# Local-global attention with a gated feed-forward: gate by min(exp, 1), global normalising on ScalarE, later last products, second buffers, weights by block

## The chip, the cores and the metric

One core of one Trainium2 chip runs the kernel. The metric is the device time of one execution, in microseconds (us). Engines are called as in the profile: PE (TensorE matmul), PEld (its weight loads), DVE (VectorE), ACT (ScalarE), POOL (GpSimd), SP (SyncE, which issues the DMAs here).

## The reference

Batch 8, 8 heads, 512 local tokens, 32 global tokens, head dimension 64; then a gated feed-forward (512 to 1536 to 512) on the 8 x 544 rows.

```python
k_all = np.concatenate([k_g, k_l], axis=2); v_all = np.concatenate([v_g, v_l], axis=2)
out_g = np.matmul(sm(scale * np.matmul(q_g, k_all.transpose(0, 1, 3, 2))), v_all)   # global rows see all keys
s_ll = np.where(np.abs(pos[:, None] - pos[None, :]) <= 32, scale * q_l @ k_l^T, -1e9)
s_l = np.concatenate([scale * q_l @ k_g^T, s_ll], axis=-1)                          # local rows: 32 global keys + a band
out_l = np.matmul(sm(s_l), np.concatenate([v_g, v_l], axis=2))
x = concat([out_g, out_l], axis=2) as (B*S, H*D)
gate = 1.0 / (1.0 + np.exp(-(x @ w_gate))); val = x @ w_val
return gate * val @ w_out
```

## The kernel before

The work is cut into chunks of tokens: two half chunks of 256 tokens for batch element 0, seven chunks of 512 for the others, and last the 256 global rows of all batch elements. `ffn_stream` is the backbone. It walks over items, one for each chunk and each of the 12 blocks of 128 hidden columns. An item is 12 matmuls into `bank_g`, 12 into `bank_v` (both L370; weights and x are split into a high and a low part, and three of the four products are taken), the gate, and one item later the matmuls into `bank_o0` to `bank_o3` (L404). The generator yields after every four matmuls; between yields a queue of events, sorted by due time, issues the attention of the next chunk and, in the first 200 us or so, the conversion of the weights from 64-bit words (`convert`, L125 to L135).

The attention of a chunk goes head by head. A head has two `local_unit`s and one `global_unit`. A local unit takes scores on PE (L229, `bank_x`), mask and row maximum on DVE (L241), exp on ACT (L244), the scaling by 1/sum (L210 or L208), transposes on PE (L260, L261, `bank_y`), a copy into `pt` (ACT L270 for the high part, DVE L271 for the low part), and the product with v on PE (L287, L288), which ACT L290, DVE L291 and POOL L292 add up. In the first chunks, where the data are not split, the copy is `pt_nat` or `pt_first` (L267) and the result is copied by L283. `x_split` (L352, L353) then makes the two parts of x. A global unit takes 32 x 512 scores (L322), min and exp (L328, L331), 1/sum (L333, L334), the scaling of `pg` (L335), five transposes on DVE (L336, L339) into `ptg`, and a split (ACT L344, POOL L345). The five products with v (L300) of a head are issued inside the next head's global unit, one after each score matmul; those of the last head of a chunk have an event of their own.

All four of `bank_g`, `bank_v`, `bank_x` and `bank_y` share four PSUM buffers (tag `att`), so PE waits for whoever read the buffer last.

The gate uses sigmoid(g) = (1 + |tanh(g/2)|) * exp(min(g, 0)) / 2:

```python
nc.scalar.activation(th, acc, AF.Tanh, scale=0.5)
nc.vector.tensor_scalar(mn, acc, 0.0, None, op0=ALU.min)   # in 12 early items Relu on ACT
nc.scalar.activation(mn, mn, AF.Exp)
nc.scalar.activation(th, th, AF.Abs)
```

The order on each engine is fixed when the program is built; the scheduler that sorts ready instructions works from the due times.

## Time and profile before

| | |
|---|---|
| median of 3 runs | 1273.19 us (1268.44 to 1275.16) |
| profiled execution, its own time | 1267.32 us |
| its span | 1265.5 us |
| mean granted TensorE clock | 0.972 |
| busy in the span | PE 94%, PEld 77%, DVE 67%, ACT 60%, POOL 47% |

A wait is printed as "engine tile line <- releaser: us in total, times, longest". In a timeline row the columns are start and duration in us, engine, line, operation, tiles and shapes, count, and in brackets the idle time just before it with what ended it. In the table of windows each engine has busy us and, in brackets, the number of its instructions.

### The profile page before, as it was taken

The numbers are of one execution on the slowest core, as the hardware profiler recorded it, in microseconds if no ns is written. First come the engines' busy times: TensorE is split into PE (matmuls) and PEld (weight loads), VectorE is DVE, ScalarE is ACT, GpSimd is POOL, SyncE is SP. The second block draws the span as 40 slices with busy tenths as digits, with TensorE's granted clock in tenths as the row PEclk, the third lists the DMA queues.
The fourth block names the chain that finished last, engine by engine and source line by source line (L and its number), as shares of the span: only waits on it lengthen the run. The fifth ranks groups of instructions, "written<-read, shape, count | busy, mean of one in ns | idle before, by whom it ended". The sixth has DMA issues, their size and how long they took to land.

```text
span 1265.5 us, 19750 instructions
## 1 busy us (share of the span) xinstructions
PE 1185.2 (94%) x6500; PEld 971.9 (77%) x6500; DVE 849.2 (67%) x2525; ACT 758.7 (60%) x1740; POOL 593.9 (47%) x630
## 2 busy tenths in 40 slices
PE   5888979989999999999999999999999999999998
PEld 4656757878788778778887778877887888788897
DVE  3787896766777577757777577757775777622232
ACT  4555556665667567656676566656765666633243
POOL 1332454553555456554556355545655456411111
PEclk9688888989999999999999999999999999999999
DMA  5665674433333333333334333333333433121133
GB/s 201 202 208 192 234 237 122 124 94 111 90 116 104 121 101 109 92 118 114 85 115 129 114 100 118 92 121 102 108 92 118 133 94 103 36 98 67 67 134 117
DMA packets 59495, 152.81 MB, mean 121 GB/s; under 512 B 6144, under 2 KB 19456, under 8 KB 59392
## 3 DMA queue, kind: packets, MB, share of 16 engines
q1 hardware_dynamic: 59392, 151.54, 38.3%
q8 instruction: 51, 0.84, 0.3%
q14 instruction: 52, 0.43, 0.1%
HBM read 136.31 MB, written 15.20 MB: 120 GB/s over the span
## 4 chain that ended last, share of the span: by engine, by line
PE 57%; DVE 18%; issue 11%; ACT 8%; POOL 4%; DMA 1%; SPq 0%; POOLq 0%; ACTq 0%; DVEq 0%
PE bank_o L404 15%; PE bank_v L370 14%; PE bank_g L370 13%; PE bank_x L229 4%; ACT s_buf L244 2%; DVE t L291 2%; PE bank_x L322 2%; DVE ptg_buf L339 2%; DVE pg_buf L335 2%; PE bank_y L260 2%; DVE s_buf L210 2%; PE bank_y L261 1%; DVE r L252 1%; PE bank_x L300 1%; PE bank_x L287 1%
## 5 line engine op out<-in xcount | busy, mean ns | idle before, releaser
L370 PE MATMUL bank_g<-xt,wg 128*128 128x512 f32 (+1 forms) x1440 | 340.9, 372 | 4.5 <-ACT xt L352 4.5
L404 PE MATMUL bank_o<-wo,hh 128*128 128x512 f32 x1224 | 330.2, 402 | 6.9 <-ACT hh L390 4.5
L370 PE MATMUL bank_v<-xt,wv 128*128 128x512 f32 (+1 forms) x1440 | 330.2, 366 | 6.3 <-DVE pt L271 6.3
L370 PEld LDWEIGHTS bank_g<-xt,wg 128*128 128x128 f32 x1440 | 242.8, 194 | 48.1 <-ACT xt L352 7.1
L370 PEld LDWEIGHTS bank_v<-xt,wv 128*128 128x128 f32 x1440 | 238.8, 190 | 46.3 <-DVE pt L271 7.8
L391 POOL TENSOR_TENSOR hh<-th,hh 128x512 fp32r<-128x512 f32 (+1 forms) x120 | 138.1, 1151 | 263.8 <-ACT hh L390 257.1
L404 PEld LDWEIGHTS bank_o<-wo,hh 128*128 128x128 f32 x1224 | 219.7, 190 | 51.0 <-ACT hh L390 5.5
L244 ACT ACTIVATE s_buf<-s_buf,nm 128x192 f32<-128x192 f32 (+1 forms) x248 | 114.0, 461 | 53.3 <-DVE nm L241 49.9
L383 DVE TENSOR_SCALAR mn<-bank_g 128x512 f32<-128x512 f32 (+1 forms) x108 | 67.0, 620 | 117.6 <-ACT th L378 117.3
L191 POOL TENSOR_TENSOR kl<-qk_raw,qk_hi 128x736 fp32r<-128x736 f32 x52 | 92.2, 1772 | 113.6 <-ACT qk_hi L190 111.5
L390 ACT CAST hh<-th 128x512 fp32r<-128x512 f32 (+1 forms) x120 | 66.5, 554 | 101.2 <-DVE th L388 99.9
L292 POOL TENSOR_TENSOR x<-t 64x256 f32<-64x256 f32 x104 | 77.1, 741 | 85.0 <-DVE t L291 82.2
L378 ACT ACTIVATE th<-bank_g 128x512 f32<-128x512 f32 (+1 forms) x120 | 64.1, 534 | 85.6 <-PE bank_g L370 81.8
L241 DVE CUSTOM_DVE_ANT_0 s_buf<-bank_x,masks 128x192 f32<-128x192 f32 (+1 forms) x248 | 82.5, 366 | 30.4 <-PE bank_x L229 28.6
L387 DVE TENSOR_TENSOR bank_v<-bank_v,mn 128x512 f32<-128x512 f32 (+1 forms) x120 | 73.2, 610 | 42.8 <-PE bank_v L370 36.5
L252 DVE TENSOR_SCALAR r<-sm 128x2 f32<-128x2 f32 x128 | 44.8, 350 | 77.5 <-ACT s_buf L244 76.6
L203 POOL TENSOR_TENSOR vhl<-v_raw,vhl 128x512 fp32r<-128x512 f32 x52 | 67.3, 1294 | 35.7 <-ACT vhl L202 34.0
L193 POOL TENSOR_TENSOR qk_hi<-qk_raw,qk_hi 64x256 fp32r<-64x256 f32 x104 | 80.2, 786 | 7.4 <-ACT qk_hi L190 2.9
L210 DVE TENSOR_SCALAR s_buf<-s_buf,r 128x224 f32<-128x224 f32 (+1 forms) x230 | 78.5, 359 | 3.4
L190 ACT CAST qk_hi<-qk_raw 128x1280 fp32r<-128x1280 f32 x52 | 65.7, 1264 | 24.9 <-PE bank_x L300 15.6
L384 ACT ACTIVATE mn<-mn 128x512 f32<-128x512 f32 (+1 forms) x108 | 63.1, 584 | 29.2 <-DVE mn L383 26.1
L339 DVE STREAM_TRANSPOSE ptg_buf<-pg_buf 32x128 f32<-32x128 f32 x256 | 77.3, 302 | 4.0
(109 smaller groups left out, 2083.4 us busy)
## 6 DMA issues: line engine op xcount, KB each, us to landing
wo<-wo_dram SPq DMA_DIRECT2D x116, 512.0 KB, 3.3
qk_raw<-in_qk_dram SPq DMA_DIRECT2D x104, 320.0 KB, 4.6
v_raw<-in_v_dram SPq DMA_DIRECT2D x52, 256.0 KB, 2.6
out_dram<-ob SPq DMA_DIRECT2D x34, 256.0 KB, 2.3
xt<-in_w_gate_dram SPq DMA_DIRECT2D x12, 512.0 KB, 4.1
xt<-in_w_val_dram SPq DMA_DIRECT2D x12, 512.0 KB, 4.2
xt<-in_w_out_dram SPq DMA_DIRECT2D x12, 512.0 KB, 4.3
v_nat<-in_v_dram SPq DMA_DIRECT2D x8, 512.0 KB, 5.7
```

The lines of the kernel that those rows point to most:

```text
L191: nc.gpsimd.tensor_tensor(kl, t[:, K0:Q1], hi[:, K0:Q1].bitcast(F32), op=ALU.subtract)
L193: nc.gpsimd.tensor_tensor(hi[64:128, r], t[64:128, r], hi[64:128, r].bitcast(F32), op=ALU.subtract)
L203: nc.gpsimd.tensor_tensor(vhl[:, :, D:2 * D], t, vhl[:, :, 0:D].bitcast(F32), op=ALU.subtract)
L210: nc.vector.tensor_scalar(out, in_, by, None, op0=ALU.mult)
L241: anchor[0] = nc.vector.tensor_tensor_reduce(out=s_sb[:, i, 0:w], in0=s_ps[:, i, 0:w], in1=masks[:, m:m + w], scale=-0.125, scalar=3.0e38, ...
L244: nc.scalar.activation(s_sb[:, i, 0:w], s_sb[:, i, 0:w], AF.Exp, bias=nm[:, i:i + 1], scale=-1.0, accum_out=sm[:, i:i + 1])
L292: nc.gpsimd.tensor_tensor(dst, t0[:, :, 0], t0[:, :, 1], op=ALU.add)
L339: nc.vector.transpose(ptg32[SG * a:SG * a + SG, 0:4], src)
L370: nc.tensor.matmul(acc, w[a][:, t, fs], xt[:, c, t, x0:x0 + ntok], start=n == 0, stop=n == 11)
L387: nc.vector.tensor_tensor(acc, acc, mn, op=ALU.mult)
L391: nc.gpsimd.tensor_tensor(hh[:, 1, 0:ntok], th, hh[:, 0, 0:ntok].bitcast(F32), op=ALU.subtract)
L404: nc.tensor.matmul(o_ps[t], ph[:, a, t * P:(t + 1) * P], pwo[:, c], start=f2 == 0 and i == 0, stop=f2 == NF - 1 and i == 2)
```

## The change

- The gate: ACT takes exp(g) straight from `bank_g` (into `ex`), and the minimum with 1 is folded into the product with the value, so the DVE min (or the ACT Relu) goes.
- The scaling of `pg` in `global_unit` goes from DVE to ACT.
- The products of the last head of a chunk come 1.25 steps of `per` later.
- `th`, `ex` and `pt` get two buffers, `ob` four, `s_buf` three. The scratch for dynamic DMAs is cut to 1024 to make room.
- The weights are laid out by block on the host, so that a block is one contiguous piece of 4 KB for each partition instead of four of 1 KB (w_gate and w_val; w_out was so before).

```diff
-    s_bufs = [const.tile([P, 2, WIN], F32, name=f"s_buf{i}") for i in range(2)]
+    s_bufs = [const.tile([P, 2, WIN], F32, name=f"s_buf{i}") for i in range(3)]
...
+    w_src = [w[f] for f in range(NF) for w in (w_gate, w_val, w_out)]
...
-            nc.sync.dma_start(st, src)
+            nc.sync.dma_start(conv_bufs[0][i % len(conv_bufs[0])], w_src[i])
...
-            s_sb = ffn.tile([P, 2, WIN], F32, name="s_first", tag="ob", bufs=2)
+            s_sb = ffn.tile([P, 2, WIN], F32, name="s_first", tag="ob", bufs=4)
...
-            s_sb = s_bufs[cnt["s"] % 2]
+            s_sb = s_bufs[cnt["s"] % 3]
...
-            pt = att.tile([P, 2, 4, P], F32R, name="pt", bufs=1)
+            pt = att.tile([P, 2, 4, P], F32R, name="pt", bufs=2)
...
-        nc.vector.tensor_scalar(pg, pg, mg[:, 3:4], None, op0=ALU.mult)
+        nc.scalar.mul(pg, pg, mg[:, 3:4])
...
-                        th = ffn.tile([P, 512], F32, name="th", bufs=1)[:, 0:ntok]
-                        mn = ffn.tile([P, 512], F32, name="mn", bufs=1)[:, 0:ntok]
+                        th = ffn.tile([P, 512], F32, name="th", bufs=2)[:, 0:ntok]
+                        ex = ffn.tile([P, 512], F32, name="ex", bufs=2)[:, 0:ntok]
                         nc.scalar.activation(th, acc, AF.Tanh, scale=0.5)
-                        if n_it < 2 * NF and n_it % 2:
-                            nc.scalar.activation(mn, acc, AF.Relu, scale=-1.0)
-                            nc.scalar.activation(mn, mn, AF.Exp, scale=-1.0)
-                        else:
-                            nc.vector.tensor_scalar(mn, acc, 0.0, None, op0=ALU.min)
-                            nc.scalar.activation(mn, mn, AF.Exp)
+                        nc.scalar.activation(ex, acc, AF.Exp)
                         nc.scalar.activation(th, th, AF.Abs)
                     else:
-                        nc.vector.tensor_tensor(acc, acc, mn, op=ALU.mult)
+                        nc.vector.scalar_tensor_tensor(acc, ex, 1.0, acc, op0=ALU.min, op1=ALU.mult)
...
-                            ob = ffn.tile([P, DM], F32, name="ob", bufs=2)
+                            ob = ffn.tile([P, DM], F32, name="ob", bufs=4)
...
-            ev.append((start + per * npu * NH, 2, lambda: list(global_products(heads[NH - 1]))))
+            ev.append((start + per * (npu * NH + 1.25), 2, lambda: list(global_products(heads[NH - 1]))))
...
-    nc = bacc.Bacc("TRN2", target_bir_lowering=False, num_devices=1)
+    nc = bacc.Bacc("TRN2", target_bir_lowering=False, num_devices=1, dynamic_dma_scratch_size=1024)
```

In the changed program the same lines have other numbers: 6 lower up to the gate (L364 is L370, L281 is L287, L294 is L300, L264 is L270, L265 is L271, L329 is L335), L376 and L377 for L387 and L388, and 11 lower behind it (L393 is L404).

The order on PE at the end of a full chunk, where the last head's products stand. Before:

```order
L370 MATMUL bank_v<-xt,wv_113 128x512 x4
L370 MATMUL bank_v<-xt,wv_112 128x512 x4
L300 MATMUL bank_x<-ptg,vhl 128x64 x5
L287 MATMUL bank_x<-pt,vhl 128x256
L288 MATMUL bank_x<-pt,vhl 128x256
...
L404 MATMUL bank_o_6237<-wo,hh 128x512
L404 MATMUL bank_o_6238<-wo,hh 128x512
```

and now, at the same place:

```order
L364 MATMUL bank_v<-xt,wv_115 128x512 x4
L281 MATMUL bank_x<-pt,vhl 128x256
L282 MATMUL bank_x<-pt,vhl 128x256
...
L364 MATMUL bank_v<-xt,wv_114 128x512 x4
L393 MATMUL bank_o_6189<-wo,hh 128x512
...
L294 MATMUL bank_x<-ptg,vhl 128x64 x5
L364 MATMUL bank_g<-xt,wg_112 128x512 x4
```

The five products moved behind the twelve `bank_o` matmuls, and the last local product (L287) moved ahead of the last four `bank_v` matmuls.

The order on ACT for the same last head, from the exp of its global scores on. Before:

```order
L331 ACTIVATE pg_buf,sg<-pg_buf,mg 32x544
L290 COPY t_9054<-bank_x 64x512
L202 CAST vhl<-v_raw 128x8x64
L270 CAST pt<-bank_y 128x512
L378 ACTIVATE th<-bank_g 128x512
L385 ACTIVATE th<-th 128x512
L384 ACTIVATE mn<-mn 128x512
L344 CAST ptg<-ptg_buf 128x5x32
```

and now:

```order
L325 ACTIVATE pg_buf,sg<-pg_buf,mg 32x544
L284 COPY t_8985<-bank_x 64x512
L329 ACTIVATE pg_buf<-pg_buf,mg 32x544
L264 CAST pt<-bank_y 128x512
L196 CAST vhl<-v_raw 128x8x64
L372 ACTIVATE th<-bank_g 128x512
L373 ACTIVATE ex<-bank_g 128x512
L374 ACTIVATE th<-th 128x512
L338 CAST ptg<-ptg_buf 128x5x32
```

The scaling of `pg` came in ahead of the cast of `pt`, the cast of the next v moved behind it, and the exponential follows the tanh at once.

## The prediction

> **What bounds the kernel now.** I read the page first: busy shares, the granted clock in the 40 slices (tenths), the chain by engine.

> ```profile
> PE 1185.2 (94%) x6500; PEld 971.9 (77%) x6500; DVE 849.2 (67%) x2525; ACT 758.7 (60%) x1740; POOL 593.9 (47%) x630
> PEclk9688888989999999999999999999999999999999
> PE 57%; DVE 18%; issue 11%; ACT 8%; POOL 4%; DMA 1%; SPq 0%; POOLq 0%; ACTq 0%; DVEq 0%
> ```

> PE is the bound: idle for 80 us in all, and only in the first nine slices throttled. None of the matmuls is removed, so what can be won is PE's idle time and its slow clock. Next the windows, to see where both lie (first 200 us, the rest of the start, one full chunk, the end without attention):

> ```profile
> 31.00:200.00 169.00, 143.82 (x775) 106.92 (x776) 139.62 (x394) 98.05 (x256) 69.86 (x56) 0.82 0.63 209
> 200.00:284.00 84.00, 76.46 (x532) 67.27 (x533) 54.57 (x185) 54.39 (x147) 45.38 (x51) 0.96 0.40 112
> 557.00:694.00 137.00, 131.15 (x713) 108.28 (x714) 100.22 (x304) 89.86 (x198) 76.08 (x82) 1.00 0.37 110
> 1107.00:1212.00 105.00, 104.44 (x463) 85.15 (x464) 27.61 (x41) 33.15 (x55) 17.79 (x15) 1.00 0.22 75
> ```

> In 31 to 200 us DVE is busy 139.6 of 169 us, nearly as long as PE, and the clock is 0.82. A full chunk loses about 6 us of 137. Last, whom PE waits for, from 0 to 200 us:

> ```profile
> PE bank_y L260 <- DVE s_buf L210: 11.5, 7, 3.0
> PE bank_x L229 <- DMA qk_nat<-in_qk_dram: 9.2, 1, 9.2
> PE bank_x L300 <- DVE ptg_buf L339: 6.5, 5, 2.1
> PE bank_o L404 <- ACT hh L390: 4.3, 2, 3.1
> PE bank_o L404 <- POOL hh L391: 1.9, 3, 0.9
> ```

> and from 200 to 1107 us:

> ```profile
> PE bank_x L300 <- POOL ptg L345: 12.0, 7, 3.8
> PE bank_x L229 <- DVE t L291: 8.7, 14, 0.7
> PE bank_v L370 <- DVE pt L271: 6.3, 12, 0.8
> PE bank_x L322 <- DVE mn L383: 4.9, 8, 0.7
> PE bank_g L370 <- ACT xt L352: 3.8, 5, 1.0
> PE bank_x L287 <- DVE pt L271: 1.7, 3, 0.7
> ```

> These repeat chunk by chunk: seven waits for `ptg` are one for each chunk with a last head, fourteen for `t` two each. The change speaks to nearly every one.

> **The change, part by part.**

> *Last products later.* One chunk end, as it is:

> ```profile
> 690.22 0.69 DVE L271 TENSOR_TENSOR pt<-bank_y,pt 128x512 fp32r<-128x512 f32 x1
> 693.31 0.52 POOL L345 TENSOR_TENSOR ptg<-ptg_buf,ptg 128x160 fp32r<-128x160 f32 x1
> 693.89 0.74 PE L300 MATMUL bank_x<-ptg,vhl 128*128 128x64 f32 x5 [1.35 <-POOL ptg L345]
> 694.47 0.36 PE L287 MATMUL bank_x<-pt,vhl 128*128 128x256 f32 x1
> 695.03 2.91 PE L404 MATMUL bank_o<-wo,hh 128*128 128x512 f32 x12
> 699.33 0.50 PE L370 MATMUL bank_g<-xt,wg 128*128 128x512 f32 x1 [0.69 <-ACT xt L352]
> ```

> `ptg` is ready at 693.83; PE was there 1.35 us before 693.89, at 692.54. Now PE first does the four local products (694.47 to 695.03, 0.56) and the twelve `bank_o` (some 2.8), so it comes to the products at 695.9, 2 us after `ptg`. That covers the pass through ACT that the scaling adds. Late next would be `pt`: L287 is reached 0.93 earlier (four of the twelve matmuls of 2.8 us now stand behind it), at 691.6, and `pt` was ready at 690.91, so 0.7 us are left. All 12.0 us of these waits go. The longest, 3.8 us, also slowed the clock:

> ```profile
> 274.50:278.50 4.00, 0.16 (x1) 0.00 (x0) 2.03 (x5) 1.47 (x5) 3.78 (x5) 0.86 0.07 26
> 278.50:284.00 5.50, 5.49 (x23) 5.30 (x24) 0.90 (x2) 1.31 (x3) 2.68 (x4) 0.50 0.49 121
> ```

> 5.5 us at 0.50 are worth 2.7. Together 14.7. The step issues no DMA, so no queue but PE's is passed. [...]

> *The wait for `xt`* (3.8): the last L287 ends 2.5 to 3 us earlier against the next chunk's `bank_g`, since waits and products no longer stand ahead of it, and L290, L291, L292, L352 follow it. A wait of 0.69 goes with that: 3.8.

> *Scaling of `pg` on ACT.* Its price on both engines, the second row for the same shape on ACT:

> ```profile
> L335 DVE TENSOR_SCALAR pg_buf<-pg_buf,mg x64: 484/749/1521, 60.1 to 1096.8; 32x544 f32<-32x544 f32 x64
> L331 ACT ACTIVATE pg_buf<-pg_buf,mg 32x544 f32<-32x544 f32 x64 | 47.7, 746 | 2.9 <-DVE mg L328 2.6
> 733.30 1.51 DVE L335 TENSOR_SCALAR pg_buf<-pg_buf,mg 32x544 f32<-32x544 f32 x1
> 734.74 0.67 DVE L291 TENSOR_TENSOR t<-bank_x,t 64x512 f32<-64x512 f32 x1
> 735.47 0.36 PE L229 MATMUL bank_x<-qk_hi 128*128 128x192 f32 x1 [0.60 <-DVE t L291]
> ```

> The scaling stands straight ahead of L291, and L229 waits for L291's buffer. With 1.5 us gone from DVE, a wait of 0.6 is gone too: 8.7 us for the fourteen. ACT gets 64 x 0.746 = 47.7 us, over the span 60% becomes 64%. [...]

> *The gate.* DVE loses L383, ACT's Exp reads PSUM instead of SBUF:

> ```profile
> L383 DVE TENSOR_SCALAR mn<-bank_g 128x512 f32<-128x512 f32 (+1 forms) x108 | 67.0, 620 | 117.6 <-ACT th L378 117.3
> L384 ACT ACTIVATE mn<-mn 128x512 f32<-128x512 f32 (+1 forms) x108 | 63.1, 584 | 29.2 <-DVE mn L383 26.1
> L387 DVE TENSOR_TENSOR bank_v<-bank_v,mn 128x512 f32<-128x512 f32 (+1 forms) x120 | 73.2, 610 | 42.8 <-PE bank_v L370 36.5
> L388 DVE SCALAR_TENSOR_TENSOR th<-th,bank_v 128x512 f32<-128x512 f32 (+1 forms) x120 | 72.0, 600 | 6.0
> ```

> L387 becomes the form of L388, 610 against 600 ns, so nothing. 67.0 us leave DVE. `bank_g` is now freed by an Exp of 0.58 right behind the Tanh, not by a min that queues on DVE: of the 4.9 us for L322 I take 3. The two waits for `pt` (8.0) hang on ACT L270 and then DVE L271: ACT's part comes later by up to 0.75, DVE's sooner. Bounds are +8 and 15 x 0.746 = 11 lost; I take 0 there and 4 us lost for all new waits behind ACT, a third of the 11, since DVE is the later one in the row above.

> *The start, 31 to 200 us.* DVE is relieved of these:

> ```profile
> L335 DVE TENSOR_SCALAR pg_buf<-pg_buf,mg 32x544 f32<-32x544 f32 x11 | 8.9, 805 | 0.0
> L383 DVE TENSOR_SCALAR mn<-bank_g 128x256 f32<-128x256 f32 x6 | 2.5, 410 | 0.4 <-ACT th L378 0.4
> ```

> 11.4 us of 139.6. The waits listed for 0 to 200 us that hang on DVE or the gate add up to 24.2 us, and the clock costs (1 - 0.82) x 143.8 = 25.9. I take half of the relief, 5.7, as shorter waits, and 5.7/24.2 of the 25.9, 6.1, as faster clock: 11.8. Bounds: 50 if all waits and the slow clock went; 13 lost if the new order of PE's first 400 rows brings two gaps of 3 us with 7 us of half clock each.

> *Weights by block and second buffers.*

> ```profile
> xt<-in_w_gate_dram SPq DMA_DIRECT2D x12, 512.0 KB, 4.1
> xt<-in_w_out_dram SPq DMA_DIRECT2D x12, 512.0 KB, 4.3
> q1 hardware_dynamic: 59392, 151.54, 38.3%
> ```

> w_out has the new shape already and lands no sooner: 0 (0 to 1 on the first wait of 9.2, behind three such loads). The smaller scratch costs nothing: all the kernel's DMAs are on one hardware queue, issued by SP. The buffers take waits from DVE, ACT and POOL that PE rarely sees: 0, at most the 1.7 of L287.

> Sum: 14.7 + 3.8 + 8.7 + 3 + 11.8 - 4 = 38.0. The profiled execution took 1267.3 (span 1265.5 and 1.8 around it), so 1229; it lies 5.9 below the median of the runs, and for a median I say 1273.2 - 38 = 1235.

> **The rivals.** (1) DVE's relief is hidden: DVE idles 37 us of a 137 us chunk (first table), and where it is waited for it may itself be waiting for ACT. Then only the moved products and `xt` pay, 18.5: 1255. Against it: L229's wait starts behind a DVE that is busy. (2) The start does better: shorter gaps no longer trip the clock, half of 24.2 and of 25.9 go (25), and the `pt` waits go too (8): 38 + 13 + 12 = 63, 1210. (3) The start's new order makes two such gaps, 13 lost instead of 11.8 won: 1260. (4) Slower: ACT's queue, with the scaling of 0.746 ahead of the `pt` cast, makes PE wait at each of 64 heads: 47.7 lost against 18.5 kept, 1302. It decides from some 25 heads on, where the slack before L287 (0.7 us at the place shown) is less than the delay. (5) The products' wait only moves to L287: 12 us less won, 1247, part of my own range.

> **How the numbers follow.** Forecast (1220 to 1248) 0.54, rival 1 0.18, rival 2 0.15, rival 3 0.08, rival 4 0.05. 1210 to 1258 leaves out half of rival 2, rival 3 and rival 4, and takes in the rest. About 0.5% (6.4 us) is what a measurement here can tell: faster 0.90, same 0.06 (the upper part of rival 3 and a weak rival 4), slower 0.04.

> **What would show it.** L300 <- `ptg`, L229 <- `t` and L370 <- `xt` gone from PE's waits after 200 us; a full chunk of 131 to 133 us instead of 136.7; DVE near 725 us busy, ACT near 800; the clock in 31 to 200 us above 0.85 and 1.00 around 280 us. I am wrong if PE waits in their place for `pt`, for `ex` or for ACT's buffer releases, or if the start has new gaps over 2 us.

## The result, and the profile after

The changed kernel was timed twice against the kernel before:

| | changed, median us | before, median us | ratio, 95% interval |
|---|---|---|---|
| first | 1222.43 (1218.76 to 1227.83) | 1274.18 | 0.9601 [0.9548, 0.9654] |
| again, five rounds | 1225.48 (1220.58 to 1227.6) | 1269.06 | 0.9644 [0.9617, 0.9671] |

It is faster by 3.6 to 4.0%, 44 to 52 us. (Each comparison timed the kernel before anew, with medians of 1267.58 to 1274.18 us, so between comparisons the ratios count, not the medians.) I had said 1235, in 1210 to 1258. The profiled execution took 1223.69 us (span 1221.4). From its page the busy shares, the granted clock by slice and the chain by engine:

```profile
PE 1180.3 (97%) x6500; PEld 970.0 (79%) x6500; DVE 751.7 (62%) x2353; ACT 768.1 (63%) x1792; POOL 588.2 (48%) x631
PEclk9797988999999999999999999999999999999999
PE 76%; DVE 8%; ACT 7%; issue 5%; POOL 2%; DMA 0%; SPq 0%; POOLq 0%; ACTq 0%; DVEq 0%
```

PE now carries 76% of the chain that ended last instead of 57%. The windows that answer to the four of before (start, rest of the start, one full chunk, end without attention):

```profile
31.00:200.00 169.00, 148.21 (x800) 109.72 (x801) 137.31 (x383) 105.04 (x272) 68.90 (x55) 0.83 0.64 210
200.00:284.00 84.00, 82.22 (x574) 70.80 (x574) 50.69 (x175) 57.98 (x150) 48.03 (x55) 1.00 0.43 126
539.00:670.00 131.00, 130.53 (x717) 108.55 (x716) 87.20 (x282) 91.66 (x207) 75.08 (x81) 1.00 0.38 114
1064.00:1169.00 105.00, 105.00 (x468) 85.69 (x468) 19.58 (x30) 30.18 (x57) 19.13 (x17) 1.00 0.21 74
```

In the window of a full chunk, 131 us, PE idles for 0.5 us instead of 6 of 137. The start looks as it did: DVE busy 137.3 us after 139.6, clock 0.83 after 0.82. Whom PE waits for, from 0 to 200 us:

```profile
PE bank_y L254 <- DVE s_buf L204: 11.9, 6, 4.3
PE bank_x L223 <- DMA qk_nat<-in_qk_dram: 7.6, 1, 7.6
PE bank_x L294 <- DVE ptg_buf L333: 5.2, 4, 2.5
PE bank_o L393 <- ACT hh L379: 1.9, 2, 1.3
```

and after 200 us, where this is the whole list:

```profile
PE bank_x L316 <- ACT ex L373: 4.4, 9, 1.1
PE bank_x L281 <- DVE pt L265: 0.4, 1, 0.4
PE bank_o L393 <- ACT hh L379: 0.2, 1, 0.2
```

The waits for `ptg`, `t`, `xt` and at `bank_v` for `pt`, 30.8 us before, are gone. One chunk end, in time:

```profile
665.64 0.28 PE L281 MATMUL bank_x<-pt,vhl 128*128 128x256 f32 x1
...
667.04 2.89 PE L393 MATMUL bank_o<-wo,hh 128*128 128x512 f32 x12
...
667.16 0.53 POOL L339 TENSOR_TENSOR ptg<-ptg_buf,ptg 128x160 fp32r<-128x160 f32 x1
...
668.66 0.62 ACT L346 CAST xt<-x 128x512 fp32r<-128x512 f32 x1 [1.62 <-POOL x L286]
...
669.77 0.64 PE L294 MATMUL bank_x<-ptg,vhl 128*128 128x64 f32 x5
670.25 2.11 PE L364 MATMUL bank_g<-xt,wg 128*128 128x512 f32 x8
```

`ptg` is there at 667.69, PE comes to the products at 669.77, 2.1 us later (I had 2), and `xt` is there at 669.28, ahead of the next `bank_g`.

**Where the gain lies.** All kernels have the same 1440 `bank_g` matmuls, so their starts are marks for the same place of the program. Counted from 0, numbers 0 to 144 are the first half chunk, 144 to 288 the second, 288 to 1152 six full chunks. In the last column stands the time in the trace's clock records at half speed between 57 and 205 us:

| kernel | 0 to 144, us | 144 to 288 | 288 to 1152 | half clock |
|---|---|---|---|---|
| before | 156.9 | 86.7 | 814.9 | 41.0 |
| changed | 153.4 | 79.6 | 783.2 | 41.0 |
| changed, again | 155.7 | 79.6 | 783.1 | 51.2 |
| before + products later | 162.1 | 82.2 | 799.1 | 61.4 |
| before + scaling on ACT | 159.5 | 87.2 | 796.2 | 54.6 |
| before + gate | 156.0 | 82.4 | 814.2 | 34.1 |
| before + second buffers | 157.2 | 86.4 | 815.1 | 41.0 |
| before + weights by block | 155.6 | 86.7 | 814.8 | 41.0 |
| before + products later + scaling | 150.9 | 83.1 | 786.2 | 41.0 |
| changed, products not later | 155.3 | 83.0 | 795.7 | 51.2 |
| changed, scaling on DVE | 160.5 | 80.4 | 796.3 | 54.6 |
| changed, old gate | 152.2 | 82.9 | 786.4 | 41.0 |
| changed, single buffers | 154.5 | 79.8 | 785.1 | 47.8 |
| changed, all of the 2^-112 scaling on ACT | 151.8 | 79.6 | 783.0 | 37.5 |

From number 144 to 1152 the change wins 901.6 - 862.8 = 38.8 us. There two profiles of the same program agree to 0.1 us; up to number 144 they differ by 2.3. So the parts can be told apart behind 144 to about a microsecond, ahead of it hardly. By the marks a full chunk takes 135.8 us before and 130.5 after (a sixth of the last stretch); the 137 and 131 above are the widths of windows set by hand.

### The profile page after: what moved, and what is told of

Its sections match the earlier page's. It is cut to its first block, busy times and chain, and to the rows that moved or that the text cites. A ratio compares the mean times of both kernels' runs of the same rounds, so it can differ in the third digit from the quotient of the medians.

```text
span 1221.4 us, 19475 instructions
## 1 busy us (share of the span) xinstructions
PE 1180.3 (97%) x6500; PEld 970.0 (79%) x6500; DVE 751.7 (62%) x2353; ACT 768.1 (63%) x1792; POOL 588.2 (48%) x631
## 3 DMA queue, kind: packets, MB, share of 16 engines
q1 hardware_dynamic: 50176, 151.54, 40.0%
## 4 chain that ended last, share of the span: by engine, by line
PE 76%; DVE 8%; ACT 7%; issue 5%; POOL 2%; DMA 0%; SPq 0%; POOLq 0%; ACTq 0%; DVEq 0%
PE bank_g L364 20%; PE bank_o L393 19%; PE bank_v L364 18%; PE bank_x L223 5%; PE bank_x L316 3%; PE bank_y L254 2%; PE bank_y L255 2%; PE bank_x L281 2%; PE bank_x L282 2%; PE bank_x L294 1%; ACT s_buf L238 1%; DVE s_buf L204 1%; DVE ptg_buf L333 1%; PE bank_x L275 1%; POOL hh L380 1%
## 5 line engine op out<-in xcount | busy, mean ns | idle before, releaser
L364 PE MATMUL bank_g<-xt,wg 128*128 128x512 f32 (+1 forms) x1440 | 339.3, 371 | 0.1
L393 PE MATMUL bank_o<-wo,hh 128*128 128x512 f32 x1224 | 330.2, 401 | 3.1 <-ACT hh L379 2.1
L364 PE MATMUL bank_v<-xt,wv 128*128 128x512 f32 (+1 forms) x1440 | 331.6, 366 | 0.0
L364 PEld LDWEIGHTS bank_g<-xt,wg 128*128 128x128 f32 x1440 | 241.3, 193 | 41.8 <-issue 5.0
L364 PEld LDWEIGHTS bank_v<-xt,wv 128*128 128x128 f32 x1440 | 237.7, 189 | 39.2 <-issue 2.3
L393 PEld LDWEIGHTS bank_o<-wo,hh 128*128 128x128 f32 x1224 | 219.7, 190 | 47.3 <-POOL hh L380 3.5
L376 DVE SCALAR_TENSOR_TENSOR bank_v<-ex,bank_v 128x512 f32<-128x512 f32 (+1 forms) x120 | 73.1, 609 | 150.3 <-PE bank_v L364 148.1
L185 POOL TENSOR_TENSOR kl<-qk_raw,qk_hi 128x736 fp32r<-128x736 f32 x52 | 92.4, 1776 | 139.6 <-ACT qk_hi L184 134.5
L235 DVE CUSTOM_DVE_ANT_0 s_buf<-bank_x,masks 128x192 f32<-128x192 f32 (+1 forms) x248 | 82.4, 366 | 35.1 <-PE bank_x L223 33.6
L204 DVE TENSOR_SCALAR s_buf<-s_buf,r 128x224 f32<-128x224 f32 (+1 forms) x230 | 89.1, 409 | 3.8
L246 DVE TENSOR_SCALAR r<-sm 128x2 f32<-128x2 f32 x128 | 38.6, 302 | 78.0 <-ACT s_buf L238 77.1
L265 DVE TENSOR_TENSOR pt<-bank_y,pt 128x512 fp32r<-128x512 f32 x104 | 71.4, 687 | 20.6 <-ACT pt L264 20.0
L285 DVE TENSOR_TENSOR t<-bank_x,t 64x512 f32<-64x512 f32 x104 | 70.7, 680 | 21.0 <-ACT t L284 17.4
## 6 DMA issues: line engine op xcount, KB each, us to landing
wo<-wo_dram SPq DMA_DIRECT2D x116, 512.0 KB, 3.3
xt<-in_w_gate_dram SPq DMA_DIRECT2D x12, 512.0 KB, 4.4
xt<-in_w_val_dram SPq DMA_DIRECT2D x12, 512.0 KB, 3.7
xt<-in_w_out_dram SPq DMA_DIRECT2D x12, 512.0 KB, 4.1
v_nat<-in_v_dram SPq DMA_DIRECT2D x8, 512.0 KB, 3.9
```

What stands on the lines that cost most here:

```text
L185: nc.gpsimd.tensor_tensor(kl, t[:, K0:Q1], hi[:, K0:Q1].bitcast(F32), op=ALU.subtract)
L204: nc.vector.tensor_scalar(out, in_, by, None, op0=ALU.mult)
L235: anchor[0] = nc.vector.tensor_tensor_reduce(out=s_sb[:, i, 0:w], in0=s_ps[:, i, 0:w], in1=masks[:, m:m + w], scale=-0.125, scalar=3.0e38, ...
L265: nc.vector.tensor_tensor(pt[:, 1], pt_ps, pt[:, 0].bitcast(F32), op=ALU.subtract)
L364: nc.tensor.matmul(acc, w[a][:, t, fs], xt[:, c, t, x0:x0 + ntok], start=n == 0, stop=n == 11)
L376: nc.vector.scalar_tensor_tensor(acc, ex, 1.0, acc, op0=ALU.min, op1=ALU.mult)
```

## The experiments

### Each part alone

**The products later.**

```diff
-            ev.append((start + per * npu * NH, 2, ...
+            ev.append((start + per * (npu * NH + 1.25), 2, ...
```

> Only the last head's products later, all else as before. Theory 1 (the part pays for itself): PE's waits for ptg (12.0 us) and for xt (3.8) go, the half clock near 280 us with them (2.7), so 18 us off, ratio 0.986. Theory 2 (the wait only moves to the last local product, which PE now reaches 0.9 us sooner while DVE still does the min and the scaling): L287 <- pt appears at each chunk end, 6 to 8 us off, ratio 0.995.

1247.78 us, ratio 0.9821 [0.9784, 0.9859]. PE's waits after 200 us:

```profile
PE bank_x L229 <- DVE t L291: 8.7, 14, 0.7
PE bank_v L370 <- DVE pt L271: 6.4, 12, 0.8
PE bank_x L322 <- DVE mn L383: 4.9, 8, 0.7
PE bank_x L287 <- DVE pt L271: 3.2, 3, 1.9
```

`ptg` and `xt` are off the list, `t` and `mn` as they were, `pt` nearly so. The part does what the prediction said of it: 20.3 us in the two stretches behind number 144 (4.5 + 15.8), for 14.7 + 3.8 = 18.5.

**The scaling of `pg` on ACT.**

```diff
-        nc.vector.tensor_scalar(pg, pg, mg[:, 3:4], None, op0=ALU.mult)
+        nc.scalar.mul(pg, pg, mg[:, 3:4])
```

> Only the scaling of pg on ACT. Theory 1: L291 comes 0.8 to 1.5 us sooner on DVE, PE's fourteen waits for t (8.7 us) go, the start gains a little: 9 to 13 us off, ratio 0.991. Theory 2 (ACT's queue is what is late): the pt cast comes 0.75 us later, the waits for pt grow as much as those for t shrink: ratio 0.998 to 1.003.

1248.38 us, 0.9836 [0.9804, 0.9868]: as much as the products, where I had less than half. After 200 us:

```profile
PE bank_x L300 <- POOL ptg L345: 12.3, 7, 3.9
PE bank_x L322 <- DVE mn L383: 9.8, 9, 2.0
PE bank_v L370 <- DVE pt L271: 2.0, 6, 0.3
PE bank_x L229 <- DVE t L291: 0.9, 2, 0.5
```

It took nearly all of `t` (8.7 to 0.9), most of `pt` at `bank_v` (6.3 to 2.0) and `xt` (3.8, off the list); `ptg` stayed, and `mn` at L322 doubled, 4.9 to 9.8.

**The gate.**

```diff
-                        nc.vector.tensor_scalar(mn, acc, 0.0, None, op0=ALU.min)
-                        nc.scalar.activation(mn, mn, AF.Exp)
+                        nc.scalar.activation(mn, acc, AF.Exp)
...
-                        nc.vector.tensor_tensor(acc, acc, mn, op=ALU.mult)
+                        nc.vector.scalar_tensor_tensor(acc, mn, 1.0, acc, op0=ALU.min, op1=ALU.mult)
```

> Only the gate: exp from the bank, min inside the product, no DVE min or ACT Relu. Theory 1 (priced in the prediction): of the waits for mn at L322 (4.9 us) some 3 go and no other: 3 to 5 us off with a little from the start, ratio 0.997. Theory 2 (the min on DVE also delayed what stands behind it): the waits for pt at bank_v (6.3 us) go as well, 10 to 12 us off, ratio 0.991.

1271.24 us, 0.9994 [0.9964, 1.0024]: no change that the times can show. After 200 us:

```profile
PE bank_x L300 <- POOL ptg L345: 11.2, 7, 1.9
PE bank_x L229 <- DVE t L291: 7.3, 12, 0.6
PE bank_g L370 <- ACT xt L352: 4.2, 4, 1.5
PE bank_x L287 <- DVE pt L271: 3.7, 11, 0.5
...
PE bank_x L322 <- ACT mn L379: 1.2, 2, 1.0
```

The waits for `mn` fall from 4.9 to 1.2, the 6.3 at `bank_v` to 1.1 (not on the rows shown), and yet six full chunks win 0.7 us. PE comes sooner to the end of the chunk and waits there for `ptg`: the seven waits are the same 11 to 12 us, and five of them are now 1.8 each, where four of these stood at 1.35 to 1.39 and one at 1.9. So part of what the gate saves is handed back while the products stand where they did: 1.7 us at these five, and 2.0 more at L287. Two such ends, at 418.8 and 555.3 us, are followed by 3.4 us at half clock in the clock records, which the kernel before doesn't have there; that costs some 3.4 us more (an estimate, half of 6.8). In all, PE's idle time in the full chunks falls by 5.6 us (29.9 to 24.3) and its busy time, with the same matmuls, rises by 4.9 (785.0 to 789.9); what makes up the rest of that rise was not traced. Between 144 and 288 the gate wins 4.3: the 3.8 us wait is cut to 1.9, and no half clock follows around 280 us. In this profile 3.1 us are lost again ahead of the first `bank_g` (it starts at 50.7 instead of 47.6 us).

**Second buffers; weights by block.**

```diff
+            pt = att.tile([P, 2, 4, P], F32R, name="pt", bufs=2)
...
+    w_src = [w[f] for f in range(NF) for w in (w_gate, w_val, w_out)]
```

> Only the second buffers (th, mn, pt two, ob four, s_buf three) and the smaller scratch. Theory 1: PE's waits stay as they are, 0 to 2 us off, ratio 0.999. Theory 2 (buffers matter, DVE and ACT no longer stop at a chunk's end for ob, and the start's order changes): 6 us or more off, ratio 0.995 or less.

> Only the weights by block. Theory 1 (priced at 0 to 1 us in the prediction): the first qk_nat lands at most 1.6 us sooner, nothing else, 0 to 2 us off, ratio 0.999. Theory 2 (4 KB pieces relieve the DMA engines in the first 200 us, and conversions start sooner): 5 us or more off, ratio 0.996 or less.

1270.69 us, 0.9998 [0.9965, 1.0032], and 1268.27 us, 0.9973 [0.9942, 1.0004]. By the table neither moves a stretch behind 144 by more than 0.3 us. By block, the loads of w_gate land in 3.6 us instead of 4.1 (medians; in the changed kernel, laid out the same, in 4.4), and nothing behind them is faster for it.

### Each part taken back from the whole

Edits as above, turned round.

> The changed kernel with the last head's products where they were. If the parts add (the part alone gave 0.982): 22 us above the changed kernel, 1245, ratio to before 0.978. If the gain overlaps with the scaling on ACT, which also makes ptg and xt come sooner at a chunk's end: 5 to 15 us above, ratio 0.965 to 0.972; then the waits for ptg are shorter than 1.35 us each.

> The changed kernel with the scaling of pg back on DVE. If the parts add (the part alone gave 0.984): 21 us above the changed kernel, 1243, ratio to before 0.976; waits for t and pt are back on PE. If the gate without the min already frees DVE enough: 5 to 10 us above, ratio 0.966.

> The changed kernel with the gate of before (min on DVE, Relu and Exp on ACT in 12 early items; second buffers kept). Theory 1 (as alone, 0.999): the same as the changed kernel within 3 us, ratio 0.961. Theory 2 (with the scaling on ACT, PE's waits for mn at L322 grew from 4.9 to 9.8 us, and the new gate is what takes these away): 5 to 8 us above, ratio 0.965.

> The changed kernel without its second buffers (th, ex, pt one buffer, ob and s_buf two, as before). Added alone to the kernel before they changed nothing (ratio 0.9998). Theory 1 (they are worth nothing here either): within 3 us of the changed kernel's 1222 us, the same waits of PE. Theory 2 (they carry the gate: with one ex, the Exp of the next item must wait until DVE has multiplied by it, and with it bank_g is freed late): bank_x L316 <- ACT ex or DVE ex grows from 4.4 to 10 us or more, and the time to 1228 to 1232 us, as with the old gate.

| taken back | median us | ratio | lost behind number 144, us |
|---|---|---|---|
| products later | 1241.49 | 0.9771 [0.9729, 0.9812] | 15.9 |
| scaling on ACT | 1243.71 | 0.9790 [0.9745, 0.9835] | 13.9 |
| gate | 1230.15 | 0.9686 [0.9644, 0.9728] | 6.5 |
| second buffers | 1227.66 | 0.9665 [0.9635, 0.9694] | 2.1 |

The waits that come back after 200 us, without the later products:

```profile
PE bank_x L294 <- POOL ptg L339: 7.0, 7, 1.7
PE bank_g L364 <- ACT xt L346: 5.0, 6, 1.6
PE bank_x L316 <- ACT ex L373: 4.4, 9, 1.1
```

with the scaling back on DVE:

```profile
PE bank_x L223 <- DVE t L285: 7.3, 12, 0.9
PE bank_x L281 <- DVE pt L265: 2.7, 6, 0.5
```

and with the old gate:

```profile
PE bank_x L316 <- DVE ex L377: 9.6, 8, 2.0
PE bank_v L364 <- DVE pt L265: 2.2, 6, 0.4
```

The first two bring back the waits that the parts alone took away, those for `ptg` at 7.0 of 12.0 us. By the ratios both come out as if the parts add (0.978 and 0.976 were expected); by the stretches each loses 4.3 to 4.4 us less than it won alone. The old gate loses 6.5 us, as its theory 2 has it.

On what the gate depends can be read off the table of stretches. In the six full chunks it is worth 0.7 us alone, 0.5 beside the scaling (796.2 to 795.7), 2.8 beside the later products (799.1 to 796.3) and 3.2 beside both; the two in the middle include the second buffers, which are worth up to 1.9 there, and the layout. So there it is the later products rather than the scaling that let the gate keep what it saves. With the second half chunk, where it wins 4.3 alone and 3.3 here, that is 5.0 us alone and 6.5 in the whole.

The second buffers are worth some 2 us, nearer to theory 1: the wait for `ex` is 4.8 us instead of 4.4, and the interval against the second timing of the changed kernel doesn't exclude zero.

### Two parts together, and the start

**Products later and scaling on ACT, nothing else.**

> The kernel before with two parts alone: the last head's products later, and the scaling of pg on ACT. Theory 1 (the two act on different waits and add; the rest of the change's gain is the gate): ratio 0.982 x 0.984 = 0.966, so some 1227 us; L300 <- ptg, L229 <- t and L370 <- xt gone, and the waits for mn at L322 left and grown, some 10 us as with the scaling alone; the full chunk 131 to 132 us. Theory 2 (they overlap: each alone already took the chunk-end waits of xt and pt): ratio 0.972 to 0.976, some 1234 us, the gate then worth more. Theory 3 (the two with the old gate collide at ACT): waits for pt or ex beyond 10 us.

1232.98 us, 0.9711 [0.9686, 0.9737]: theory 1 had 0.966, theory 2 0.972 to 0.976, and the second is the nearer. Behind 144 it wins 32.3 us, where the parts alone win 20.3 and 18.2: 6.2 us overlap, of which the waits for `xt`, which both take away, are 3.8. The old gate's wait is the first on its list after 200 us:

```profile
PE bank_x L322 <- DVE mn L383: 9.8, 9, 2.0
PE bank_v L370 <- DVE pt L271: 2.0, 6, 0.3
```

From this kernel to the whole change another 6.5 us go, the same as the gate's loss when it is taken back.

**The 18 multiplications of the weight conversion that are left on DVE, put on ACT.**

```diff
-REBASE = "vs"
+REBASE = "s"
```

> The changed kernel, with the 18 multiplications by 2^-112 of the weight conversion that are left on DVE (L124, some 0.43 to 1.38 us each, 11 us in the first 182 us) put on ACT (the other 18 are there already, 0.67 us each). It asks of the start term, which came out at a third of what I predicted, whether DVE's load sets the start. Theory 1 (DVE's load bounds the start, as the prediction had it: relief of a us gives half of it in waits and as much again in clock): 11 us of relief win 8 to 12, so 1211 to 1215 us, and the mark at the 144th bank_g matmul comes 5 us or more earlier. Theory 2 (the start is bound by the chain of the conversion and the scaling, and by PE's own throttled clock; DVE's relief is hidden): within 3 us of 1222, DVE 11 us less busy, clock in 31 to 200 us still 0.81 to 0.84.

1216.19 us (1211.4 to 1217.99), 0.9574 [0.9547, 0.9601], the fastest kernel here: 6.2 us below the first median of the changed kernel and 9.3 below the second, whose interval of ratios it doesn't touch (it does the first's). The start in its windows, and the longest waits there:

```profile
31.00:200.00 169.00, 148.76 (x824) 111.97 (x824) 127.83 (x373) 116.35 (x296) 71.68 (x58) 0.85 0.66 212
```

```profile
PE bank_x L223 <- DMA qk_nat<-in_qk_dram: 7.9, 1, 7.9
PE bank_y L254 <- DVE s_buf L204: 5.2, 4, 2.5
PE bank_x L294 <- DVE ptg_buf L333: 4.8, 6, 1.9
...
PE bank_y L254 <- DVE mg L327: 2.6, 1, 2.6
```

DVE is 9.5 us less busy and the waits for `s_buf` fall from 11.9 to 5.2; another 2.6 at the same matmul is now put down to DVE's L327. Behind number 144 nothing changes. The mark itself comes at 195.0 us, after 200.0 and 204.1 in the changed kernel, and 3.4 and 5.2 us of that lie ahead of the first `bank_g` (43.2 after 46.6 and 48.4). So taking load off DVE in the start pays, which is nearer to theory 1, though the time is 1 us above its range. How much of it comes through shorter waits stays open: the time at half clock is lower too, 37.5 us, and no run separates the two.

**The changed kernel once more.**

> The changed kernel itself, timed once more in five rounds. Its first ratio, 0.9601, has an interval of 0.9548 to 0.9654, too wide to tell it from the kernel with single buffers (0.9665, 0.9635 to 0.9694) and from the one with the weight scaling off DVE (0.9574, 0.9547 to 0.9601). Theory 1 (the second buffers are worth nothing, the relief of DVE in the start a little): 0.963 to 0.966. Theory 2 (the buffers are worth 5 us or more, the relief nothing): 0.957 to 0.961. Its second profile also tells how far the start varies between two executions of the same program: the mark at the 144th bank_g matmul, 200.0 us in the first, within 5 us of it.

0.9644, inside theory 1's range; the mark at number 144 came at 204.1 us instead of 200.0. Of the second buffers it is right. Its "a little" for the relief of DVE is too small: from 0.9644 to the 0.9574 of the kernel above is 0.7%.

## Why the prediction held, step by step

| term | predicted, us | measured behind number 144: alone / taken back |
|---|---|---|
| products later + `xt` | 14.7 + 3.8 | 20.3 / 15.9 |
| scaling on ACT | 8.7 | 18.2 / 13.9 |
| gate | 3 | 5.0 / 6.5 |
| new waits behind ACT | -4 | in the rows above |
| second buffers, weights by block | 0 | 0 / 2.1; 0 |
| start | 11.8 | up to number 144: 3.5 and 1.2 (two profiles) |

*Products and `xt`*: right in mechanism, place and size, and the chunk end shows the 2 us that I had worked out. *Rival 5*, that the wait moves to L287: one wait of 0.4 (L281) in the whole change, 1.5 us in the part alone (1.7 to 3.2).

*Scaling*: right that the 14 waits for `t` hang on it, and half the size. I counted only the queue straight behind L335. The same 0.5 to 1.5 us also stood ahead of every later step on DVE, L271 among them, so 4.3 of the `pt` waits went with it, and `xt`. I had those waits at 0, since ACT's part comes later. It does, but on DVE more was saved than ACT lost. These rows add up to less than the 18.2 measured even before the 4.9 more for `mn` come off; the trace has no shorter pauses that could hold the rest. In the six full chunks PE's idle time falls by 12.3 us (29.9 to 17.6), and its busy time, with the same matmuls, by 6.3 (785.0 to 778.7); the ends of matmuls are modelled in the profile, and I did not trace this part further.

*Its price on ACT*: the prediction's rows have 749 ns on DVE (median) and 746 on ACT (mean). A longer scaling would have shown in the waits for `ptg_buf`. They went from 6.5 to 5.2 in the whole change and to 2.4 with the move alone, which won 1.6%, and the durations on ACT hardly vary:

```profile
L329 ACT ACTIVATE pg_buf<-pg_buf,mg x64: 731/747/753, 58.6 to 1054.8; 32x544 f32<-32x544 f32 x64
```

The 484 to 1521 ns on DVE that the prediction showed are not noise, as the last section shows.

*Gate and the -4*: both are real and cancel. The scaling on ACT makes the wait at L322 grow by 4.9 (4.9 to 9.8) as long as `bank_g` is freed by a min on DVE; the new gate brings it to 4.4. I had put the 3 us to the gate's account by itself. Alone it does shorten that wait, by 3.7 us, but the full chunks win only 0.7 and the times show nothing that can be told from zero. *Rival 4*, ACT's queue, would have shown as waits for `pt` at 64 heads; there is one.

*The start* is the step that failed: 11.8 predicted, 3.5 and 1.2 seen. Its first half, 5.7 us of shorter waits, may be there: the slow clock's cost taken off (half of the last column, an estimate), 156.9 becomes 136.4 for the kernel before and 153.4 and 155.7 become 132.9 and 130.1. Its second half, a clock that improves in proportion to the waits, is wrong: the time at half clock stayed at 41.0 us in one profile and rose to 51.2 in the other. One chain that PE waits for holds nothing of what the change takes off DVE. It ends PE's longest wait in the start but for the first load:

```profile
182.90 1.26 POOL L129 TENSOR_TENSOR wg<-xt,wg 128x512 fp32r<-128x512 f32 x1 [2.36 <-ACT wg L128]
182.95 1.33 DVE L204 TENSOR_SCALAR s_buf<-s_buf,r 128x192 f32<-128x192 f32 x1
...
184.33 0.47 PE L254 MATMUL bank_y<-ident,s_buf 128*128 128x128 f32 x1 [4.26 <-DVE s_buf L204]
```

Ahead of this L204, from 179.5 us on, DVE works through five steps of the weight conversion, and none of the 11.4 us that the change takes off DVE stood there. L204 itself takes 1.33 us beside POOL's L129; the mean with POOL idle is 0.32. The edit of `REBASE` takes away one of the five steps (L124), and pays.

*The sum*: 38.0, and 38.8 behind number 144 alone. The steady terms were 12.6 too low (26.2), the start some 8 to 11 too high. That the sum came near is partly luck, since these two errors cancel: in the profiled executions the time fell by 43.6 us (1267.32 to 1223.69), and the point, 1235, stands 9.5 and 12.6 us above the two medians. Of the signs that the prediction named, the waits, the full chunk (130.5 us) and the clock around 280 us came out so or nearly so; DVE's 751.7 us (725 expected), ACT's 768.1 (800) and the clock of the start, 0.83 (above 0.85), did not.

## What to carry to other kernels

A wait that is removed early in a stage can be paid back at the next fixed meeting point, unless that one is moved too (the gate in the full chunks: 0.7 us with the products where they stood, 3.2 with them moved): look for the last wait of each stage first, and judge the earlier ones only together with it. When an operation leaves an engine, count every wait for that engine's later results, not only the one right behind. And price an operation by its minimum, median and maximum: the wide spread of the scaling on DVE, 484 to 1521 ns, went with POOL's work (489 ns in the mean with none running at its start, 1029 beside it).

## What the runs showed of the hardware

**DVE behind POOL.** In the kernel before, 44 of the 64 scalings at L335 start while a POOL operation is running; they take 1029 ns in the mean. The 20 others take 489. Of the 44, each of over 0.5 us ends 0.29 to 0.30 us after that POOL operation, like the one shown in the prediction (733.30, 1.51 us), beside which this ran:

```profile
733.22 1.30 POOL L203 TENSOR_TENSOR vhl<-v_raw,vhl 128x512 fp32r<-128x512 f32 x1
```

733.22 + 1.30 = 734.52, and L335 ends at 734.81. A POOL operation that began later, during the scaling, did not lengthen it (two such, 484 and 491 ns). The same shows for L252, 128 x 2 elements: 166 ns in the mean with POOL idle at its start, 594 beside POOL. The operations here that read PSUM and the transposes take nearly the same time beside POOL as without it: L271 670 and 686 ns, L291 667 and 675, L387 594 and 617 (two shapes), L339 302 and 303. Over the median of the free ones that is 23.7 us in L335 and 23.4 in L252 in the kernel before. It is read from the trace; no run changed POOL's work to test it. The 484 ns of the prediction's row are thus the price with no POOL operation running at the start; why the others end with POOL was not shown.

```profile
98.90:109.10 10.20, 8.49 (x59) 5.84 (x58) 7.35 (x25) 6.70 (x20) 3.64 (x3) 1.00 0.60 199
109.10:119.40 10.30, 9.42 (x33) 7.06 (x33) 8.53 (x26) 5.24 (x13) 3.02 (x3) 0.50 0.51 178
```

PE is idle for 1.7 us in the first, with no wait over 1.41, and then has half the clock for 10.2 us. So a single long wait, like the 3.8 us ahead of the half clock at 278.5 us that the prediction shows, is not the only thing that the slow clock follows here: this stretch came after short pauses alone. Cut into windows of 3.41 us on the steps of the clock records (25 to 1100 us of all 14 profiles, 4108 windows at full clock), half clock followed directly on each of the 46 windows in which PE was busy for less than 47%, none of the 3828 with more than 81%, and 47 of the 234 in between (in the profiles of before and changed alone: 7 of 7, none of 546, 5 of 38). The last window ahead of the stretch shown has 60%. What decides in between was not found. Between the 14 profiles the time at half clock in the start lies between 34.1 and 61.4 us, and the first half chunk between 150.9 and 162.1, longest where the slow time is longest. The mark at number 144 came at 200.0 and 204.1 us in the two profiles of the changed kernel, so a change in the start of under 5 us can't be read from one profile.
